# Weight tiles of 512 decoded in place, a 16-pair lag of the MoE behind the scores, three r tiles, and an output product moved ahead of a chunk's first product

## The chip, the cores and the metric

The kernel runs on one core of a Trainium2 chip. The metric is device time in microseconds (us), the median of three runs. In the text PE is TensorE (matmuls), PEld its weight loads, DVE is VectorE, ACT is ScalarE, POOL is GpSimd and SP is SyncE, whose queue issues every DMA of this kernel. Each engine works through its own instructions in order, and semaphores make one wait for another.

## The reference

Attention with squared ReLU in place of a softmax, gated by `u`, and behind it a mixture-of-experts block with one expert (RMS norm, SiLU gate, value projection, output projection):

```python
def _attn_ref(u, v, z):                 # batch 4, seq 3008, d_model 256, d_qk 64
    scores = (1.0 / S) * np.matmul(z, z.transpose(0, 2, 1))
    attn = np.maximum(scores, 0.0) ** 2
    return (u * np.matmul(attn, v)).astype(np.float32)

def _moe_ref(x, w_gate, w_val, w_out, rms_g):     # 12032 tokens, d_ff 1536
    rms = np.sqrt(np.mean(x * x, axis=-1, keepdims=True) + 1e-06)
    xn = x / rms * rms_g
    g = xn @ w_gate
    silu = g * (1.0 / (1.0 + np.exp(-g)))
    return (silu * (xn @ w_val) @ w_out).astype(np.float32)
```

The three weight matrices are float64 in the inputs; `u`, `v`, `z` are float32.

## The kernel before

**Tiling.** Of each batch's 3008 tokens, 512 make a chunk (five of 512 and one of 448: 24 chunks in all), and 128 make a k-tile (24, the last one half full). A *step* is one pair of chunk and k-tile; there are 576, and one loop runs over them (line 590). All products are made of two-part numbers, high and low: a step's attention product is six matmuls into `po` (`emit_av`, lines 353, 354, 358), a score is two (`emit_s`, lines 297, 298).

**A step.** The scores of step i+3 (LA = 3 ahead) go to PSUM; ACT takes the ReLU into a tile `r` (line 300; two such tiles). Then either ACT squares it twice, once rounded into `H` and once in place (lines 315, 316), or DVE multiplies it by the PSUM scores (line 302) and ACT rounds it into `H` (318); `is_square` says which. DVE subtracts to get the low part `L` (321). The scores are symmetric: for blocks that `keeps` names, ACT writes the square's halves out (334) and a later chunk reads them back turned, by a DMA transpose into tiles `T`, and needs no score matmuls for them.

**Chunk border.** Behind a chunk's last step, DVE multiplies `po` by `u` (`emit_gate`, 375). The next chunk's first product writes the same two `po` banks, so it waits for that. Thirteen small stages of the RMS norm (`norm_jobs`) follow, one in each step.

**MoE.** It trails the scores by `NK // 2 + SKEW` pairs of steps, SKEW = 8: in an even step six matmuls of the gate projection (`emit_g`, 464 to 467) and ACT's SiLU into the one `s` tile (474), in an odd step six of the value projection, then DVE's product `s` (483), ACT's `hH` (484) and DVE's `hL` (485). The output product `py` of the pair before (`emit_y`, 498 to 500) comes in even steps behind `emit_av`. There are 288 such pairs; those that are left when attention ends make the tail.

**Weights.** They come as pairs of 32-bit words (the float64's halves) in 36 tiles of 256 columns, 256 KB each. ACT takes a square (130), DVE runs three operations on the high words (134 to 138) and two more (143, 145), ACT rounds (146), and POOL makes the low part (147, 148). `load_w` finds a tile for each load among places that are free by then. They are planned from step 1 on, one in three steps, then in two, then in each.

**Order.** All instructions stand in program order as the loop emits them; `stages` and `loads` are lists by step. The loads of `v` and `z` use the `raw` ring (three tiles), in the first chunks with other tiles as well, and are planned four or five steps ahead.

Of the kernel before, what the change touches and what calls it, by code (L numbers as in the profile page):

```python
# [24 lines left out]

WC = 256
LEAST = 1.125 * 2.0 ** -15
# [3 lines left out]
def kernel(  # L31
# [25 lines left out]
    LA = 3  # L57
    SKEW = 8

    AHEAD = 5  # L60
    RAW = 3
    SCALE = 1.0 / S
# [35 lines left out]


    wraw_tags = [f"x{a}{d}{k}" for k in range(2) for a in "hl" for d in range(ND)] + ["raw"] * RAW  # L100
    w_queue = []

    def load_w(i):

        while w_queue and w_queue[0][0] <= i + AHEAD:
            at, load = w_queue[0]

            free = [t for t in wraw_tags if t == "raw" or at + 2 < (int(t[-1]) + 1) * NK + 11]
            if not free:
                assert at > i + 1, "no room"  # L110
                return
            w_queue.pop(0)
            load(free[0])

    def prep_w(src, hi, lo):

        tiles = {}

        def load(tag):
            wraw_tags.remove(tag)
            raw = work.tile([P, WC, 2], U32, tag=tag, name="wraw", bufs=RAW if tag == "raw" else 1)
            nc.sync.dma_start(out=raw.rearrange("p a b -> p (a b)"), in_=src.bitcast(U32))
            tiles["raw"] = raw, tag

        def magnitude(i):

            tiles["t"] = work.tile([P, WC], U32, tag="wt", name="wt", bufs=3)
            nc.scalar.activation(lo, f32(tiles["raw"][0][:, :, 1]), AF.Square)  # L130

        def upper(i):
            wh, t = tiles["raw"][0][:, :, 1], tiles["t"]
            nc.vector.tensor_scalar(t, wh, 3, 0x3FFFFFF8, op0=ALU.logical_shift_left, op1=ALU.bitwise_and)
            yield
            nc.vector.scalar_tensor_tensor(t, wh, 0xC0000000, t, op0=ALU.bitwise_and, op1=ALU.bitwise_or)
            yield
            nc.vector.scalar_tensor_tensor(f32(t), f32(lo), LEAST * LEAST, f32(t), op0=ALU.is_ge, op1=ALU.mult)

        def lower(i):  # L140
            (raw, tag), t = tiles["raw"], tiles["t"]
            wl, m = raw[:, :, 0], raw[:, :, 1]
            nc.vector.tensor_scalar(m, t, 0xFF800000, None, op0=ALU.bitwise_and)
            yield
            nc.vector.scalar_tensor_tensor(f32(m), wl, 2.0 ** -52, f32(m), op0=ALU.mult, op1=ALU.mult)
            nc.scalar.copy(hi, f32(t))
            nc.gpsimd.tensor_tensor(f32(t), f32(t), f32(hi), op=ALU.subtract)
            nc.gpsimd.tensor_tensor(lo, f32(t), f32(m), op=ALU.add)
            wraw_tags.append(tag)
            wraw_tags.sort(key=lambda t: t[-1])  # L150

        return load, [magnitude, upper, lower]


# [4 lines left out]

    rings = {True: ["raw", "T", "hH", "T", "hL"], False: ["raw"]}  # L160

    def new_raw(first):

        ring = rings[first]
        ring.append(ring.pop(0))
        if ring[-1] == "T":
            return work.tile([P, 2 * CH], F32, tag="T", name="raw", bufs=3)[:, :CH]
        return work.tile([P, CH], F32, tag=ring[-1], name="raw", bufs=RAW if ring[-1] == "raw" else 1)

# [19 lines left out]
    def prep_stat(b, c):  # L189
        t0 = c * CH  # L190
        n = min(CH, S - t0)
        m = n + TAIL if n < CH else n
        lo = slice(DQK, P)
        tiles = {}

        def load(i):
            raw = tiles["raw"] = new_raw(b == 0)
            nc.sync.dma_start(out=raw[:, :n], in_=zT2[:, b * S + t0:b * S + t0 + n])
            if n < m:
                nc.sync.dma_start(out=raw[:, n:m], in_=zT2[:, (b + 1) * S - TAIL:(b + 1) * S])  # L200

        def high(i):
            raw = tiles["raw"]
            z = keep.tile([P, CH], F32R, tag=f"zst{c}", name=f"zst{c}")
            nc.scalar.copy(z[:DQK, :m], raw[:DQK, :m])
            nc.vector.tensor_copy(z[lo, :m], raw[lo, :m])
            zst[b, c] = z

        def low(i):
            z = zst[b, c]  # L210
            nc.vector.tensor_tensor(z[lo, :m], tiles["raw"][lo, :m], f32(z[lo, :m]), op=ALU.subtract)

        return load, [high, low]

# [20 lines left out]
    def prep_v(b, g):  # L235
# [12 lines left out]

        def high(i):
            hi = vh[b, g] = keep.tile([P, 2, D], F32R, tag=f"vh{g}", name=f"vh{g}")  # L250
            nc.vector.tensor_copy(hi, tiles["raw"])

        def low(i):
            lo = vl[b, g] = keep.tile([P, 2, D], F32R, tag=f"vl{g}", name=f"vl{g}")
            nc.vector.tensor_tensor(lo, tiles["raw"], f32(vh[b, g]), op=ALU.subtract)  # L255

        return load, [high, low]

# [8 lines left out]
    def keeps(b, c, kc):  # L267


        return (b * NC + c) * NK + 4 * kc >= NK + 2 * SKEW  # L270

# [15 lines left out]
    def emit_s(i):  # L287
# [10 lines left out]
        nc.tensor.matmul(ps[:, :n], z[:, ks], ml[:, :n], start=False, stop=True)  # L298
        a = work.tile([P, CH], F32, tag="r", name="r", bufs=2)
        nc.scalar.activation(a[:, :n], ps[:, :n], AF.Relu)  # L300
# [4 lines left out]
    def is_square(i):  # L305

        return i < 2 * NK + 2 * SKEW and i % 4 != 3

    def emit_l(i):
# [19 lines left out]
        if kc > c and keeps(b, c, kc):  # L329
            if kt % 4 == 0:  # L330
                kept[b, kc, c] = dram.tile([2 * CH, CH], U16, tag=f"kept{kc}{c}", name=f"kept{kc}{c}")
            m = P if kt < NK - 1 else TAIL
            halves = work.tile([P, 2, CH], U16, tag="halves", name="halves", bufs=2)
            nc.scalar.copy(halves[:m], a[:m].bitcast(U16).rearrange("p (q h) -> p h q", h=2))  # L334
            r0 = 2 * (kt % 4) * P
            nc.sync.dma_start(
                out=kept[b, kc, c][r0:r0 + 2 * m, :].rearrange("(p h) q -> p h q", h=2), in_=halves[:m]
            )
# [138 lines left out]
    def emit_v(ci, f):  # L477
        n = chunks[ci][3]
        ps = proj(ci, f, wvh, wvl)
        h = moe["s"]  # L480
        hi = work.tile([P, CH], F32R, tag="hH", name="hH")
        lo = work.tile([P, CH], F32R, tag="hL", name="hL")
        nc.vector.tensor_tensor(h[:, :n], ps[:, :n], h[:, :n], op=ALU.mult)  # L483
# [6 lines left out]
    def emit_y(ci, f):  # L490
# [10 lines left out]
        if f == NF - 1:  # L501
            for d in range(ND):
                y = work.tile([P, CH], F32, tag=f"q{d}", name="y")
                if d == 0:
# [7 lines left out]

    nsteps = len(steps)
    loads = defaultdict(list)
# [8 lines left out]
    for g in range(NK // 2):  # L523
        if g % 2 == 0 and g // 2 + 1 < NC:
            plan(prep_stat(0, g // 2 + 1), 2 * g - 2, AHEAD)
        if g > 1:
            plan(prep_v(0, g), 2 * g - 3, AHEAD)
    at = 1
    for j in range(DFF // WC):
        js = slice(j * WC, (j + 1) * WC)  # L530
        group = []
        for src, hi, lo in ((w_gate, wgh, wgl), (w_val, wvh, wvl)):
            for d in range(ND):
                group.append((src[d * P:(d + 1) * P, js], hi[:, d, js], lo[:, d, js]))
        for f in range(j * WC // P, (j + 1) * WC // P):
            group.append((w_out[f * P:(f + 1) * P, :], woh[:, f, :], wol[:, f, :]))
        for w in group:
            load, parts = prep_w(*w)
            w_queue.append((at, load))
            for k, part in enumerate(parts):  # L540
                stages[at + k].append(part)
            at += 3 if at < NK else 2 if at < NK + 2 * SKEW - 2 else 1
    for ci in range(1, len(chunks)):

        first = next(i for i in range(ci * NK, (ci + 1) * NK) if not is_turned(i))
        plan(prep_mov(ci), max(ci * NK - LA - 1, first - LA - 4), 4)
    for i in range(0, len(steps), 2):
        if is_turned(i):
            loads[i - LA - 3].append(lambda at, i=i: load_turned(i))
    for b in range(1, batch):  # L550
        first = b * NC * NK
        for c in range(NC):
            plan(prep_stat(b, c), first - NK + 4 * c + 3, 4)
        for g in range(NK // 2):
            plan(prep_v(b, g), first - NK + 2 * g + 2, 4)

# [13 lines left out]
    with tc.manual_schedule():  # L570
# [4 lines left out]
        for i in sorted(k for k in loads if k < 0):  # L575
            run(loads, i)
        load_w(0)
        prep_const()
# [11 lines left out]
        for i in range(nsteps + 2 * (SKEW + NF + 1)):  # L590
# [11 lines left out]
            run(loads, i)  # L602
            load_w(i)
            m = moe_at(fs)
            if m:
                if i % 2 == 0:
                    emit_g(*m)
                else:
                    emit_v(*m)
            if i < nsteps:  # L610
                emit_av(i)
            m = moe_at(fs - 1)
            if m and i % 2 == 0:
                emit_y(*m)
# [39 lines left out]
```

## Time and profile before

| | before |
|---|---|
| median of 3 runs | 2247.09 us (2246.83 to 2247.13) |
| profiled execution | 2247.23 us, its span 2245.5 us |
| granted PE clock over the span | 0.995 |
| matmuls | 9368 |
| DMA | 166.78 MB, mean 74 GB/s |
| ACT's largest wait for a matmul chain: `hH` for `s` | 567.1 us |

The busy shares overlap. A busy PE is not one at its peak, since each matmul's recorded time covers part of the next one's; how far apart matmuls start says more. Idle time counts only on the engine that sets the pace of its stretch. Names such as `po<-H,vh` mean: tile `po` is written, from `H` and `vh`.

### The profile page before, as it was taken

Reading aid. Unit: us, or ns where it says so; the run is one execution under the profiler, and the core shown is the slowest. Engines: PE = TensorE matmul, PEld = TensorE weight load, DVE = VectorE, ACT = ScalarE, POOL = GpSimd, SP = SyncE. Lnnn points to the kernel's source line nnn. Section 1 sums busy time; section 2 is a strip of 40 time slices with the busy share of each in tenths; the row PEclk is TensorE's granted clock in tenths of the full one; section 3 lists DMA queues with packets and bytes.
Section 4 is the critical chain, followed back from the end, with each engine's and each line's share of the span. In section 5 each row is a group of like instructions: output and inputs, shape, how many; then the busy total and the mean of one; then the engine's idle time right before and its main releaser. Section 6 shows DMA issues by size and latency. Waiting matters only on the chain.

```text
span 2245.5 us, 25802 instructions
## 1 busy us (share of the span) xinstructions
PE 2180.1 (97%) x9368; PEld 1748.5 (78%) x9368; DVE 1321.8 (59%) x2416; ACT 1167.9 (52%) x1994; POOL 61.6 (3%) x76
## 2 busy tenths in 40 slices
PE   7789999999999999999999999999999999999998
PEld 4456787888888878788788787788888877877876
DVE  7668655567555555557656555556755565555442
ACT  6676645444656455344566463544465655544332
POOL 1233000000000000000000000000000000000000
PEclk9999999999999999999999999999999999999999
DMA  4131303152223142334131332415222314133200
GB/s 137 38 101 43 96 15 86 47 115 70 88 56 110 43 101 61 78 91 109 63 97 57 77 93 48 109 47 119 82 80 64 114 38 106 53 82 77 63 0 18
DMA packets 280016, 166.78 MB, mean 74 GB/s; under 512 B 218640, under 2 KB 234128, under 8 KB 279888
## 3 DMA queue, kind: packets, MB, share of 16 engines
q1 hardware_dynamic: 279888, 165.13, 28.0%
q8 instruction: 73, 1.20, 0.2%
q14 instruction: 55, 0.45, 0.1%
HBM read 46.60 MB, written 65.40 MB: 50 GB/s over the span
## 4 chain that ended last, share of the span: by engine, by line
PE 86%; DVE 6%; ACT 5%; issue 2%; DMA 0%; POOL 0%; DVEq 0%; ACTq 0%; SPq 0%; POOLq 0%
PE ps L464 11%; PE ps L465 10%; PE ps L467 10%; PE po L353 10%; PE po L354 10%; PE po L358 10%; PE py L498 6%; PE py L500 6%; PE py L499 6%; PE ps L297 3%; PE ps L298 3%; DVE L L321 2%; DVE s L483 1%; ACT hH L484 1%; ACT r L300 1%
## 5 line engine op out<-in xcount | busy, mean ns | idle before, releaser
L353 PE MATMUL po<-H,vh 128*128 128x512 f32 (+1 forms) x1152 | 458.9, 398 | 23.6 <-DVE ux L375 13.4
L484 ACT CAST hH<-s 128x512 fp32r<-128x512 f32 (+1 forms) x288 | 176.4, 612 | 567.1 <-DVE s L483 567.1
L354 PE MATMUL po<-H,vl 128*128 128x512 f32 (+1 forms) x1152 | 452.2, 393 | 0.3 <-DVE vl L255 0.3
L302 DVE TENSOR_TENSOR r<-ps,r 128x512 f32<-128x512 f32 (+1 forms) x316 | 216.6, 686 | 322.5 <-ACT r L300 321.8
L300 ACT ACTIVATE r<-ps 128x512 f32<-128x512 f32 (+1 forms) x364 | 216.4, 595 | 345.5 <-PE ps L298 244.8
L358 PE MATMUL po<-L,vh 128*128 128x512 f32 (+1 forms) x1104 | 344.1, 393 | 10.1 <-DVE L L321 10.1
L483 DVE TENSOR_TENSOR s<-ps,s 128x512 f32<-128x512 f32 (+1 forms) x288 | 194.6, 676 | 237.5 <-PE ps L467 237.1
L485 DVE TENSOR_TENSOR hL<-s,hH 128x512 fp32r<-128x512 f32 (+1 forms) x288 | 196.2, 681 | 198.9 <-ACT hH L484 198.9
L353 PEld LDWEIGHTS po<-H,vh 128*128 128x128 f32 x1152 | 217.4, 189 | 94.8 <-ACT H L318 22.1
L321 DVE TENSOR_TENSOR L<-r,H 128x512 fp32r<-128x512 f32 (+1 forms) x340 | 237.7, 699 | 46.9 <-ACT r L316 23.8
L358 PEld LDWEIGHTS po<-L,vh 128*128 128x128 f32 x1104 | 205.8, 188 | 63.8 <-DVE L L321 20.2
L354 PEld LDWEIGHTS po<-H,vl 128*128 128x128 f32 x1152 | 217.5, 189 | 45.9 <-DVE vl L255 1.5
L498 PE MATMUL py<-hH,woh 128*128 128x512 f32 (+1 forms) x576 | 228.6, 397 | 14.4 <-ACT hH L484 13.6
L500 PE MATMUL py<-hL,woh 128*128 128x512 f32 (+1 forms) x576 | 228.4, 396 | 0.0
L464 PE MATMUL ps<-xh,wgh 128*128 128x512 f32 (+1 forms) x576 | 226.2, 393 | 1.6 <-ACT s L474 1.6
L464 PE MATMUL ps<-xh,wvh 128*128 128x512 f32 (+1 forms) x576 | 224.6, 390 | 0.0
L465 PE MATMUL ps<-xh,wvl 128*128 128x512 f32 (+1 forms) x576 | 224.6, 390 | 0.0
L334 ACT COPY halves<-r 128x1024 uint16<-128x1024 uint16 x212 | 222.1, 1047 | 4.4 <-DMA kept<-halves 4.2
L499 PE MATMUL py<-hH,wol 128*128 128x512 f32 (+1 forms) x576 | 224.1, 389 | 0.0
L465 PE MATMUL ps<-xh,wgl 128*128 128x512 f32 (+1 forms) x576 | 224.0, 389 | 0.0
L474 ACT ACTIVATE s<-ps 128x512 f32<-128x512 f32 (+1 forms) x288 | 169.9, 590 | 101.8 <-PE ps L467 74.1
L318 ACT CAST H<-r 128x512 fp32r<-128x512 f32 (+1 forms) x316 | 192.5, 609 | 0.6 <-DVE small L409 0.3
(81 smaller groups left out, 2713.0 us busy)
## 6 DMA issues: line engine op xcount, KB each, us to landing
kept<-halves SPq DMA_DIRECT2D x193, 256.0 KB, 2.0
raw<-in_v SPq DMA_DIRECT2D x44, 256.0 KB, 3.3
ux<-in_uT SPq DMA_DIRECT2D x40, 256.0 KB, 2.8
out_T<-y SPq DMA_DIRECT2D x40, 256.0 KB, 2.0
raw<-in_zT SPq DMA_DIRECT2D x39, 256.0 KB, 2.9
wraw<-in_w_gate SPq DMA_DIRECT2D x12, 256.0 KB, 3.1
wraw<-in_w_val SPq DMA_DIRECT2D x12, 256.0 KB, 2.7
wraw<-in_w_out SPq DMA_DIRECT2D x12, 256.0 KB, 3.1
```

The source lines that it names most:

```text
L300: nc.scalar.activation(a[:, :n], ps[:, :n], AF.Relu)
L321: nc.vector.tensor_tensor(lo[:, :n], a[:, :n], f32(hi[:, :n]), op=ALU.subtract)
L334: nc.scalar.copy(halves[:m], a[:m].bitcast(U16).rearrange("p (q h) -> p h q", h=2))
L353: nc.tensor.matmul(po[d][:, :n], wh[:, j, ds], hi[:, :n], start=(kt == 0), stop=False)
L354: nc.tensor.matmul(po[d][:, :n], wl[:, j, ds], hi[:, :n], start=False, stop=(lo is None))
L358: nc.tensor.matmul(po[d][:, :n], wh[:, j, ds], lo[:, :n], start=False, stop=False)
L464: nc.tensor.matmul(ps[:, :n], hi[:, d, fs], xsplit[ci, d][0][:, :n], start=(d == 0), stop=False)
L465: nc.tensor.matmul(ps[:, :n], lo[:, d, fs], xsplit[ci, d][0][:, :n], start=False, stop=False)
L467: nc.tensor.matmul(ps[:, :n], hi[:, d, fs], xsplit[ci, d][1][:, :n], start=False, stop=(d == ND - 1))
L498: nc.tensor.matmul(py[d][:, :n], woh[:, f, ds], hi[:, :n], start=(f == 0), stop=False)
L499: nc.tensor.matmul(py[d][:, :n], wol[:, f, ds], hi[:, :n], start=False, stop=False)
L500: nc.tensor.matmul(py[d][:, :n], woh[:, f, ds], lo[:, :n], start=False, stop=(f == NF - 1))
```

## The change

- **Weights**: 18 tiles of 512 columns (512 KB each) in place of 36 of 256, decoded in the tile itself, at a stride of two words, with one scratch tile `wt`. They take turns on the three `T` tiles and are loaded three steps ahead. The first is due at step 4; one follows every 5 steps up to step 59, then every 2 up to step 71.
- **SKEW** goes from 8 to 16: the MoE begins at step 56 in place of 40, and 28 pairs stand in the tail in place of 20. `keeps` begins at NK + 3·SKEW = 72 in place of 40, which takes out five blocks of batch 0 (20 scores are computed that had been read back turned). `is_square` covers steps up to 80 and two of three steps, in place of 64 and three of four.
- **Tiles**: `r` three in place of two; `raw` two in place of three, with loads of later batches planned two steps ahead in place of four; `halves` and `y` share two tiles; from the tail on `hH` and `hL` use the three `H` and `L` tiles.
- **Splits** of `v` and `z` take one step in place of two.
- **Output product**: in a chunk's first step `emit_y` comes ahead of `emit_av`; in the tail it comes behind the value projection in place of the gate projection.

```diff
-WC = 256
+WC = 512
...
-    SKEW = 8
+    SKEW = 16
...
-    RAW = 3
+    RAW = 2
...
-    wraw_tags = [f"x{a}{d}{k}" for k in range(2) for a in "hl" for d in range(ND)] + ["raw"] * RAW
-    def load_w(i):
...
     def prep_w(src, hi, lo):
+        a, b = hi.shape[1:]
...
-        def load(tag):
-            wraw_tags.remove(tag)
-            raw = work.tile([P, WC, 2], U32, tag=tag, name="wraw", bufs=RAW if tag == "raw" else 1)
-            nc.sync.dma_start(out=raw.rearrange("p a b -> p (a b)"), in_=src.bitcast(U32))
-            tiles["raw"] = raw, tag
+        def load(i):
+            raw = work.tile([P, a, b, 2], U32, tag="T", name="wraw", bufs=3)
+            nc.sync.dma_start(out=raw.rearrange("p a b c -> p a (b c)"), in_=src.bitcast(U32))
+            tiles["wl"], tiles["wh"] = raw[:, :, :, 0], raw[:, :, :, 1]
+        def new_t():
+            return work.tile([P, WC], U32, tag="wt", name="wt").rearrange("p (a b) -> p a b", a=a)
         def magnitude(i):
-            tiles["t"] = work.tile([P, WC], U32, tag="wt", name="wt", bufs=3)
-            nc.scalar.activation(lo, f32(tiles["raw"][0][:, :, 1]), AF.Square)
+            nc.scalar.activation(hi, f32(tiles["wh"]), AF.Square)
         def upper(i):
-            wh, t = tiles["raw"][0][:, :, 1], tiles["t"]
+            wh, t = tiles["wh"], new_t()
...
-            nc.vector.scalar_tensor_tensor(t, wh, 0xC0000000, t, op0=ALU.bitwise_and, op1=ALU.bitwise_or)
-            yield
-            nc.vector.scalar_tensor_tensor(f32(t), f32(lo), LEAST * LEAST, f32(t), op0=ALU.is_ge, op1=ALU.mult)
+            nc.vector.scalar_tensor_tensor(wh, wh, 0xC0000000, t, op0=ALU.bitwise_and, op1=ALU.bitwise_or)
+            yield
+            nc.vector.scalar_tensor_tensor(f32(wh), f32(hi), LEAST * LEAST, f32(wh), op0=ALU.is_ge, op1=ALU.mult)
         def lower(i):
-            (raw, tag), t = tiles["raw"], tiles["t"]
-            wl, m = raw[:, :, 0], raw[:, :, 1]
-            nc.vector.tensor_scalar(m, t, 0xFF800000, None, op0=ALU.bitwise_and)
-            yield
-            nc.vector.scalar_tensor_tensor(f32(m), wl, 2.0 ** -52, f32(m), op0=ALU.mult, op1=ALU.mult)
-            nc.scalar.copy(hi, f32(t))
-            nc.gpsimd.tensor_tensor(f32(t), f32(t), f32(hi), op=ALU.subtract)
-            nc.gpsimd.tensor_tensor(lo, f32(t), f32(m), op=ALU.add)
-            wraw_tags.append(tag)
-            wraw_tags.sort(key=lambda t: t[-1])
+            wh, wl, t = tiles["wh"], tiles["wl"], new_t()
+            nc.vector.tensor_scalar(t, wh, 0xFF800000, None, op0=ALU.bitwise_and)
+            yield
+            nc.vector.scalar_tensor_tensor(f32(wl), wl, 2.0 ** -52, f32(t), op0=ALU.mult, op1=ALU.mult)
+            nc.scalar.copy(hi, f32(wh))
+            nc.gpsimd.tensor_tensor(f32(wh), f32(wh), f32(hi), op=ALU.subtract)
+            nc.gpsimd.tensor_tensor(lo, f32(wh), f32(wl), op=ALU.add)
...
-    rings = {True: ["raw", "T", "hH", "T", "hL"], False: ["raw"]}
+    rings = {True: ["raw", "hH", "raw", "hL"], False: ["raw"]}
     def new_raw(first):
...
-        if ring[-1] == "T":
-            return work.tile([P, 2 * CH], F32, tag="T", name="raw", bufs=3)[:, :CH]
...
     def prep_mov(ci):
...
     def keeps(b, c, kc):
-        return (b * NC + c) * NK + 4 * kc >= NK + 2 * SKEW
+        return (b * NC + c) * NK + 4 * kc >= NK + 3 * SKEW
     def is_turned(i):
...
-        a = work.tile([P, CH], F32, tag="r", name="r", bufs=2)
+        a = work.tile([P, CH], F32, tag="r", name="r", bufs=3)
...
     def is_square(i):
-        return i < 2 * NK + 2 * SKEW and i % 4 != 3
+        return i < 2 * NK + 2 * SKEW and i % 3 != 2
     def emit_l(i):
...
-            halves = work.tile([P, 2, CH], U16, tag="halves", name="halves", bufs=2)
+            halves = work.tile([P, 2, CH], U16, tag="out", name="halves", bufs=2)
...
-        hi = work.tile([P, CH], F32R, tag="hH", name="hH")
-        lo = work.tile([P, CH], F32R, tag="hL", name="hL")
+        own = 2 * (ci * NF + f + NK // 2 + SKEW) < nsteps
+        hi = work.tile([P, CH], F32R, tag="hH" if own else "H", name="hH", bufs=1 if own else LA)
+        lo = work.tile([P, CH], F32R, tag="hL" if own else "L", name="hL", bufs=1 if own else LA)
...
-                y = work.tile([P, CH], F32, tag=f"q{d}", name="y")
+                y = work.tile([P, CH], F32, tag="out", name="y", bufs=2)
...
-    nsteps = len(steps)
...
-            plan(prep_stat(0, g // 2 + 1), 2 * g - 2, AHEAD)
+            plan(prep_stat(0, g // 2 + 1), 2 * g - 1, AHEAD)
...
-            plan(prep_v(0, g), 2 * g - 3, AHEAD)
-    at = 1
+            plan(prep_v(0, g), 2 * g - 2, AHEAD)
+    at = 4
...
+        fs = slice(j * WC // P, (j + 1) * WC // P)
...
-                group.append((src[d * P:(d + 1) * P, js], hi[:, d, js], lo[:, d, js]))
-        for f in range(j * WC // P, (j + 1) * WC // P):
-            group.append((w_out[f * P:(f + 1) * P, :], woh[:, f, :], wol[:, f, :]))
+                group.append((src[d * P:(d + 1) * P, js].unsqueeze(1), hi[:, d:d + 1, js], lo[:, d:d + 1, js]))
+        for f in range(fs.start, fs.stop, 2):
+            rows = w_out[f * P:(f + 2) * P, :].rearrange("(a p) d -> p a d", p=P)
+            group.append((rows, woh[:, f:f + 2, :], wol[:, f:f + 2, :]))
...
-            load, parts = prep_w(*w)
-            w_queue.append((at, load))
-            for k, part in enumerate(parts):
-                stages[at + k].append(part)
-            at += 3 if at < NK else 2 if at < NK + 2 * SKEW - 2 else 1
+            plan(prep_w(*w), at, 3)
+            at += 5 if at < NK + 2 * SKEW else 2
...
-        plan(prep_mov(ci), max(ci * NK - LA - 1, first - LA - 4), 4)
+        plan(prep_mov(ci), max(ci * NK - LA - 1, first - LA - 4), 2)
...
-            plan(prep_stat(b, c), first - NK + 4 * c + 3, 4)
+            plan(prep_stat(b, c), first - NK + 4 * c + 3, 2)
...
-            plan(prep_v(b, g), first - NK + 2 * g + 2, 4)
+            plan(prep_v(b, g), first - NK + 2 * g + 2, 2)
     def moe_at(fs):
...
-        load_w(0)
...
-            load_w(i)
...
+            m = moe_at(fs - 1)
+            y_first = i < nsteps and kt == 0
+            if m and y_first:
+                emit_y(*m)
...
-            m = moe_at(fs - 1)
-            if m and i % 2 == 0:
+            if m and not y_first and i % 2 == (0 if i < nsteps else 1):
...
```

How it moves instructions, at three places. First PE at a chunk's border in the middle of the program (`ps<-xl,wgh` ends the gate projection, `po` is the new chunk's first product, `py` the output product). Before:

```order
L467 MATMUL ps<-xl_10445,wgh 128x512
L353 MATMUL po_10881<-H,vh_8531 128x512
L354 MATMUL po_10881<-H,vl_8566 128x512
L353 MATMUL po_10882<-H,vh_8531 128x512
L354 MATMUL po_10882<-H,vl_8566 128x512
L358 MATMUL po_10881<-L,vh_8531 128x512
L358 MATMUL po_10882<-L,vh_8531 128x512
L498 MATMUL py_10711<-hH,woh 128x512
```

And with the change:

```order
L444 MATMUL ps<-xl_9273,wgh 128x448
L477 MATMUL py_10048<-hH,woh 128x448
L478 MATMUL py_10048<-hH,wol 128x448
L479 MATMUL py_10048<-hL,woh 128x448
L477 MATMUL py_10049<-hH,woh 128x448
L478 MATMUL py_10049<-hH,wol 128x448
L479 MATMUL py_10049<-hL,woh 128x448
L330 MATMUL po_10500<-H,vh_8142 128x512
L331 MATMUL po_10500<-H,vl_8144 128x512
```

The six `py` matmuls stand between the gate projection and the first writer of `po`.

Second, PE in the tail (`wgh` is the gate projection, `wvh` and `wvl` the value projection). Before:

```order
L467 MATMUL ps<-xl_18436,wgh 128x448
L467 MATMUL ps<-xl_18439,wgh 128x448
L498 MATMUL py_18551<-hH,woh 128x448
L499 MATMUL py_18551<-hH,wol 128x448
L500 MATMUL py_18551<-hL,woh 128x448
L498 MATMUL py_18552<-hH,woh 128x448
L499 MATMUL py_18552<-hH,wol 128x448
L500 MATMUL py_18552<-hL,woh 128x448
L464 MATMUL ps<-xh_18435,wvh 128x448
```

And with the change:

```order
L444 MATMUL ps<-xl_18049,wgh 128x448
L444 MATMUL ps<-xl_18052,wgh 128x448
L441 MATMUL ps<-xh_18048,wvh 128x448
L442 MATMUL ps<-xh_18048,wvl 128x448
L441 MATMUL ps<-xh_18051,wvh 128x448
L442 MATMUL ps<-xh_18051,wvl 128x448
L444 MATMUL ps<-xl_18049,wvh 128x448
L444 MATMUL ps<-xl_18052,wvh 128x448
L477 MATMUL py_18400<-hH,woh 128x448
```

`py` has moved behind the value projection.

Third, DVE in the first chunk, around the decoding of the first weight tile (`wt` and `wraw`; `L` and `r` belong to the scores, `zst`, `vh` and `vl` to the splits). Before:

```order
L134 TENSOR_SCALAR wt<-wraw 128x256
L136 SCALAR_TENSOR_TENSOR wt<-wraw,wt 128x256
L138 SCALAR_TENSOR_TENSOR wt<-wgl,wt 128x256
L321 TENSOR_TENSOR L<-r,H 128x512
L211 TENSOR_TENSOR zst_196<-raw,zst_196 64x512
L251 CAST vh_225<-raw 128x512
L143 TENSOR_SCALAR wraw<-wt 128x256
L145 SCALAR_TENSOR_TENSOR wraw<-wraw 128x256
```

And with the change:

```order
L121 TENSOR_SCALAR wt<-wraw 128x512
L123 SCALAR_TENSOR_TENSOR wraw<-wraw,wt 128x512
L125 SCALAR_TENSOR_TENSOR wraw<-wgh,wraw 128x512
L298 TENSOR_TENSOR L<-r,H 128x512
L230 CAST vh_276<-raw 128x512
L232 TENSOR_TENSOR vl_278<-raw,vh_276 128x512
L129 TENSOR_SCALAR wt<-wraw 128x512
L131 SCALAR_TENSOR_TENSOR wraw<-wraw,wt 128x512
```

The same five operations are twice as wide, write into the raw tile, and both halves of a `v` split stand together.

More of the change, by code (lines that the diff above doesn't have):

```diff
@@ L76 @@
     steps = [(ci, kt) for ci in range(len(chunks)) for kt in range(NK)]
+    nsteps = len(steps)
     def f32(ap):
@@ L97, in prep_const @@
         nc.sync.dma_start(out=fold_sb, in_=fold)
-    wraw_tags = [f"x{a}{d}{k}" for k in range(2) for a in "hl" for d in range(ND)] + ["raw"] * RAW
-    w_queue = []
-    def load_w(i):
[L105 to L113, printed above, removed]
@@ L200, in load, with split @@
                 nc.sync.dma_start(out=raw[:, n:m], in_=zT2[:, (b + 1) * S - TAIL:(b + 1) * S])
-        def high(i):
+        def split(i):
             raw = tiles["raw"]
@@ L206, in high @@
             nc.vector.tensor_copy(z[lo, :m], raw[lo, :m])
+            nc.vector.tensor_tensor(z[lo, :m], raw[lo, :m], f32(z[lo, :m]), op=ALU.subtract)
             zst[b, c] = z
[L209 to L213, printed above, removed]
+        return load, [split]
     def prep_first():
@@ L247, in load, with split @@
                     nc.sync.dma_start(out=view[h * TAIL:(h + 1) * TAIL, 1, :], in_=v[r0 + P:r0 + P + TAIL, :])
-        def high(i):
+        def split(i):
             hi = vh[b, g] = keep.tile([P, 2, D], F32R, tag=f"vh{g}", name=f"vh{g}")
             nc.vector.tensor_copy(hi, tiles["raw"])
-        def low(i):
             lo = vl[b, g] = keep.tile([P, 2, D], F32R, tag=f"vl{g}", name=f"vl{g}")
             nc.vector.tensor_tensor(lo, tiles["raw"], f32(vh[b, g]), op=ALU.subtract)
-        return load, [high, low]
+        return load, [split]
     att = {}
```

## The prediction

> **What bounds the kernel now.** I read the page first, then busy time by stretches, then groups and waits inside the slow stretch, then the timeline at a chunk's border and at the end.
>
> ```profile
> PE 2180.1 (97%) x9368; PEld 1748.5 (78%) x9368; DVE 1321.8 (59%) x2416; ACT 1167.9 (52%) x1994; POOL 61.6 (3%) x76
> PE 86%; DVE 6%; ACT 5%; issue 2%; DMA 0%; POOL 0%; DVEq 0%; ACTq 0%; SPq 0%; POOLq 0%
> ```
>
> PE's 97% is no measure of how full it is, because a matmul's busy time overlaps the next one's. The spacing of starts is the measure:
>
> ```profile
> 2151.16 0.39 PE L464 MATMUL ps<-xh,wvh 128*128 128x512 f32 x1
> 2151.39 0.40 PE L465 MATMUL ps<-xh,wvl 128*128 128x512 f32 x1
> ...
> 75.20 0.63 PE L354 MATMUL po<-H,vl 128*128 128x512 f32 x1
> 75.63 0.63 PE L353 MATMUL po<-H,vh 128*128 128x512 f32 x1
> ```
>
> A full 512-wide matmul occupies 0.233 us at full clock, and 0.43 us where the clock was halved. With 0.233 I weigh five stretches, cut at the first `po` product of steps 0, 24, 40 and 64 and near the end of attention:
>
> ```profile
> core 0: us, PE busy (x) PEld busy (x) DVE busy (x) ACT busy (x) POOL busy (x), PEclk, DMA share, GB/s
> 8.87:83.13 74.26, 59.00 (x192) 34.82 (x191) 53.41 (x102) 47.05 (x89) 12.69 (x14) 0.95 0.26 84
> 83.13:132.28 49.15, 37.49 (x137) 24.38 (x138) 34.48 (x78) 30.80 (x60) 11.37 (x14) 0.97 0.17 53
> 132.28:248.96 116.68, 103.28 (x404) 76.92 (x403) 93.58 (x192) 80.96 (x155) 37.31 (x44) 0.96 0.24 76
> 248.96:2158.50 1909.54, 1897.33 (x8307) 1551.75 (x8306) 1105.75 (x1982) 981.37 (x1645) 0.00 (x0) 1.00 0.30 76
> ```
>
> 192 matmuls (24 steps of 8) are worth 44.7 us and took 74.3: 29.5 over. The next two rows are 49.2 − 31.9 = 17.2 and 116.7 − 94.1 = 22.5 over. So 69 us are lost before step 64. The long fourth row has 8307 matmuls at 0.230 us each, with the 448-wide ones among them: PE is full there, and only a small regular wait is left. The kernel is therefore bound by PE, except in its first 250 us, at chunk borders, and in its tail.
>
> In the first 40 steps (3.09 us each, with 1.87 us of matmuls) neither DVE (87.9 of 123.4 us) nor ACT (77.9) is full. They wait for each other:
>
> ```profile
> L300 ACT ACTIVATE r<-ps 128x512 f32<-128x512 f32 x25 | 15.0, 599 | 26.6 <-DVE L L321 25.5 <-PE ps L298 1.1
> L321 DVE TENSOR_TENSOR L<-r,H 128x512 fp32r<-128x512 f32 x24 | 18.1, 753 | 14.9 <-ACT r L316 12.2 <-ACT H L318 2.4
> ACT r L300 <- DVE L L321: 43.5, 39, 3.1
> PE ps L297 <- DVE mh L181: 4.5, 1, 4.5
> ```
>
> The first two rows are groups of steps 0–23, the last two are waits of steps 0–39. With two `r` tiles, the ReLU of a step has to wait until DVE has taken `L` from the `r` of two steps earlier: 43.5 us in 39 waits.
>
> **The change part by part.** The profiled execution took 2247.23 us (span 2245.5), 0.14 above the median shown; the sum starts from 2247.2.
>
> *(1) The start: three `r` tiles, bigger weight tiles, MoE 16 steps later.* The third `r` tile moves that wait a whole step back, so I let it go. What is late next is DVE itself. A weight tile costs DVE two `tensor_scalar` and three `scalar_tensor_tensor`, at these prices:
>
> ```profile
> L136 DVE SCALAR_TENSOR_TENSOR wt<-wraw,wt 128x256 uint32<-128x256 uint32 x8 | 3.4, 425 | 0.3
> L134 DVE TENSOR_SCALAR wt<-wraw 128x256 uint32<-128x256 uint32 x8 | 2.3, 288 | 0.0
> L181 DVE TENSOR_SCALAR mh<-raw 128x512 fp32r<-128x512 f32 x19 | 8.0, 419 | 0.0
> L183 DVE SCALAR_TENSOR_TENSOR ml<-raw,mh 128x512 fp32r<-128x512 f32 x19 | 13.1, 692 | 1.4
> L136 DVE SCALAR_TENSOR_TENSOR wt<-wraw,wt 128x256 uint32<-128x256 uint32 x21 | 13.1, 623 | 0.0
> 180.00:200.00 20.00, 18.20 (x77) 13.54 (x76) 18.23 (x38) 11.86 (x26) 7.67 (x9) 1.00 0.19 62
> ```
>
> At 256 wide that is 2 × 0.288 + 3 × 0.425 = 1.85 us; at 512 wide, by the rows of `mh` and `ml`, 2 × 0.42 + 3 × 0.69 = 2.91. No row shows the 512-wide form written in place at a stride of two words. From below it is bounded by 2.91. From above I take the stretched form, since the fifth row (steps 40–63) shows the same instruction at 623 ns where DVE and POOL are both loaded: 2 × 0.42 + 3 × 1.02 = 3.9. In the sparse start I use 2.91, as the 256-wide forms, two of them strided, run unstretched there.
>
> DVE's work in the new steps 0–55: the 87.9 us of the old steps 0–39, less 15 old tiles (27.8), plus 16 more `L` (11.0), about 9 more `r` products as `is_square` and its span change (6.0), one more `mh`/`ml` pair (1.1), most of chunk 1's gate and norm (7), plus 11 new tiles (32.0): 117 us. ACT has less. The last row shows how full DVE gets where it leads: 91%. That gives 129 us. Run step by step without any slack (a heavy step of DVE never overlapping a heavy one of ACT) I come to about 148. I take 140, nearer the middle, because LA lets engines drift by a step or two but the border at step 24 (the 4.5 us wait for `mh`) keeps part of its cost. 56 steps are 448 matmuls, 104.4 us: 35.6 over.
>
> Steps 56–72 then carry MoE and the last 7 weight tiles. DVE: 17 `L` (11.7), 6 `r` products (4), 7 tiles at 2.9 to 3.9 (20 to 27), 17 MoE operations (11.6), norms (4): 52 to 59 us. PE: 17 steps of about 17 matmuls, 67 us. PE leads, with little room; I allow 5. Together 40.6 over in place of 69.3: **−28.7**, between −40 (129 us and no loss behind) and −17 (148 us, 8 behind).
>
> POOL's two operations double in width and halve in number; ACT's too. They lie beside this. The weight loads grow to 512 KB and are issued three steps ahead:
>
> ```profile
> wraw<-in_w_gate SPq DMA_DIRECT2D x12, 256.0 KB, 3.1
> ```
>
> Three steps are 7 us in the start, and twice the 3.1 us of a 256 KB load is 6.2 at most, so I cost them at nothing; were each 3 us late, DVE would have L and v work to go on with.
>
> *(2) The output product ahead of a chunk's first product.*
>
> ```profile
> PE po L353 <- DVE ux L375: 13.4, 19, 1.3
> 1262.03 0.69 DVE L485 TENSOR_TENSOR hL<-s,hH 128x512 fp32r<-128x512 f32 x1 [0.69 <-ACT hH L484]
> 1262.25 0.64 PE L467 MATMUL ps<-xl,wgh 128*128 128x512 f32 x2
> 1262.64 1.28 DVE L375 TENSOR_TENSOR ux<-po,ux 128x512 f32<-128x512 f32 x2
> 1263.47 0.47 PE L353 MATMUL po<-H,vh 128*128 128x512 f32 x1 [0.58 <-DVE ux L375]
> ```
>
> DVE takes the gate only after `hL`; PE runs out of matmuls at 1262.72 and starts `po` at 1263.47. Six `py` matmuls put in there take 1.4 us, to 1264.1, past the gate's first half. Their own input `hL` is done at 1262.72, and the first reader of it stands third. So the wait goes: **−13.4**. Borders 24 and 48 have no MoE work and keep theirs. If `py` waited as long as `po` does now, the term would be zero.
>
> *(3) The tail: `py` behind both projections.*
>
> ```profile
> 2199.93 0.62 DVE L483 TENSOR_TENSOR s<-ps,s 128x448 f32<-128x448 f32 x1 [2.44 <-PE ps L467]
> 2201.19 0.62 DVE L485 TENSOR_TENSOR hL<-s,hH 128x448 fp32r<-128x448 f32 x1 [0.63 <-ACT hH L484]
> 2201.21 0.47 PE L498 MATMUL py<-hH,woh 128*128 128x448 f32 x1 [0.18 <-ACT hH L484]
> 2201.91 0.55 ACT L474 ACTIVATE s<-ps 128x448 f32<-128x448 f32 x1 [0.75 <-DVE hL L485]
> 2204.27 0.62 DVE L483 TENSOR_TENSOR s<-ps,s 128x448 f32<-128x448 f32 x1 [2.46 <-PE ps L467]
> 2238.03 0.36 PE L465 MATMUL ps<-xh,wvl 128*128 128x448 f32 x1
> 2238.23 0.56 PE L467 MATMUL ps<-xl,wvh 128*128 128x448 f32 x2
> 2240.18 0.47 PE L498 MATMUL py<-hH,woh 128*128 128x448 f32 x1 [1.38 <-ACT hH L484]
> ```
>
> A pair takes 4.34 us where its 18 matmuls need 18 × 0.200 = 3.6, since `py` stands right behind the next gate product and needs an `hH` that is just being made. 12 pairs lose 0.74 and 8 wider ones about 0.5; the last loses 1 more: 13.9. In the new order `py` comes one more projection and one more `py` later (2.4 us), beyond `hL`. The loop over the one `s` tile (L483 to the end of L474) takes 2.5 us and fits into 3.6. There are 28 pairs now in place of 20, all at PE's pace. The very last `py` still waits some 0.4: **−13.5**, and zero at worst.
>
> *(4) Fewer kept scores.* `keeps` asks for 72 where it asked for 40, so five blocks of batch 0 are computed and not turned: 40 more matmuls, 24 of 512 and 16 of 448 (0.233 and 0.200 us), all in the stretch where PE is full: **+8.8**. ACT loses 20 `halves` copies, DVE gains 20 products; both are half idle there.
>
> Sum: 2247.2 − 28.7 − 13.4 − 13.5 + 8.8 = **2200**.
>
> **A rule against the row.** Short spells of half clock lie in the start; one is in this row:
>
> ```profile
> 120.00:130.00 10.00, 6.75 (x21) 4.18 (x22) 6.23 (x12) 5.37 (x12) 2.97 (x4) 0.83 0.33 106
> 121.11 0.50 PE L353 MATMUL po<-H,vh 128*128 128x512 f32 x1 [1.67 <-ACT H L315]
> ```
>
> The Trainium skill, "TensorE: Matmul & The Clock Gate", section "HAM oscillation — how this bites in real kernels", has it that only PE gaps above about 3.4 us throttle the array. By that rule shorter gaps would end all spells and (1) would sit nearer its −40. The trace differs: here the clock fell with no PE wait above 1.67 us in the row, so I count no gain from it.
>
> **Rivals.**
> - *The start stays as it is* (13%): ACT and DVE remain in lockstep for other reasons, and 56 steps go at 3.09 us, 173 us, 69 over. Term (1) is zero: 2229. For it: three waits of different kinds stand in that stretch. Against it: 43.5 us of one kind, with DVE at 71% and ACT at 63%.
> - *`py` or its tile inherits the border's wait* (6%): term (2) is zero: 2213.
> - *Half clock through the attention-only steps* (3%): 8 × 0.43 = 3.4 us a step, 190 us in place of 140: 2250, no change. Against it: PE is busier there than before, and the clock was 0.95 and 0.97.
> - *Slower: late `v` and `z` loads at the three changes of batch* (5%). `raw` has two tiles in place of three and loads are planned two steps ahead in place of four, on SP's queue, where a load waiting for its tile holds up all behind it. One takes 3.3 us:
>
> ```profile
> raw<-in_v SPq DMA_DIRECT2D x44, 256.0 KB, 3.3
> ```
>
> 54 loads exposed by half of that cost 89 us: 2289. It decides from 0.96 us each (52 us over the forecast). Two steps of 3.73 us (1909.5 us over 512 steps) leave 4.1 us beyond the landing, so a load is exposed only where its tile comes free a whole step after it was asked for; by the due times that is one load at each change. Hence the small chance.
>
> **How the numbers follow.** The forecast has 73% and its own range 2184 to 2214 (term (1) from −40 to −17, and a few us for borders and tail). Reaching into the first rival, 2184 to 2225 leaves out about 2 in 10: most of that rival, the last two, and a little below. This kernel's runs can tell about 0.2%, 4.5 us, from no change. Faster: forecast, first two rivals, 92%; same 3%; slower 5%.
>
> **What would show it.** Right: the wait of `r` for `L` nearly gone; DVE near 85–90% busy in the first 56 steps, with step 56 near 150 us; no wait of `po` for `ux` after step 72; tail pairs at 3.6 us. Wrong: step 56 near 180 us; `py` waiting at borders for `hL`; DVE waiting for `raw` in a batch's last chunk; PE clock near 0.5 early.

## The result, and the profile after

The changed kernel takes 2186.56 us (median of 4 runs, 2185.81 to 2187.04) against 2247.11 us; the ratio is 0.9731, 95% interval 0.9714 to 0.9747. That is 60.6 us less, where 47 were forecast. The profiled execution took 2186.13 us. Its page begins:

```profile
span 2184.4 us, 25522 instructions
PE 2152.9 (99%) x9408; PEld 1763.3 (81%) x9408; DVE 1321.7 (61%) x2340; ACT 1161.1 (53%) x1964; POOL 55.2 (3%) x40
PE 92%; DVE 5%; ACT 1%; issue 1%; DMA 1%; SPq 0%; DVEq 0%; ACTq 0%
```

PE has 40 matmuls more, and its share of the chain that ended last went from 86% to 92%. Busy time by stretches, cut at the first `po` product of steps 0, 24, 56 and 72 and near the end of attention (columns as before):

```profile
8.90:69.33 60.43, 49.05 (x191) 35.89 (x191) 55.70 (x87) 45.13 (x82) 12.47 (x8) 0.97 0.39 122
69.33:146.08 76.75, 66.75 (x265) 50.78 (x265) 66.47 (x115) 58.59 (x105) 18.47 (x12) 0.96 0.17 57
146.08:210.96 64.88, 64.13 (x272) 50.08 (x270) 53.56 (x82) 42.38 (x76) 20.87 (x14) 1.00 0.17 54
210.96:2066.00 1855.04, 1854.46 (x8151) 1525.68 (x8150) 1092.99 (x1966) 973.47 (x1633) 3.14 (x2) 1.00 0.29 75
```

At 0.233 us a matmul the first three are 15.9, 15.0 and 1.5 us over, 32.4 together; before, 69.3 were lost by step 64. DVE is busy for 122.2 of the 137.2 us of steps 0 to 55, 89%. Step 56 began at 146.1 us (about 149 forecast). In the fourth row PE is busy for all but 0.6 us. The start's two groups (steps 0 to 55), and the wait of `po` for the gate, over the whole run:

```profile
L277 ACT ACTIVATE r<-ps 128x512 f32<-128x512 f32 x58 | 34.3, 592 | 24.0 <-DVE L L298 13.7 <-PE ps L275 9.8
L298 DVE TENSOR_TENSOR L<-r,H 128x512 fp32r<-128x512 f32 x56 | 50.5, 909 | 10.7 <-ACT r L293 6.7 <-ACT H L295 3.9
PE po L330 <- DVE ux L352: 1.8, 1, 1.8
```

ACT's idle time for `L` fell from 43.5 us in 40 steps to 13.7 in 56, and of 19 waits of `po` for the gate one is left, before the MoE begins. One number was not expected: an `L` takes 909 ns here, where it takes 690 elsewhere.

In the tail a pair of 448 columns now takes 3.60 us, which is 18 matmuls of 0.200 us, as `s` shows on the timeline:

```profile
2141.81 0.62 DVE L462 TENSOR_TENSOR s<-ps,s 128x448 f32<-128x448 f32 x1 [0.94 <-PE ps L444]
2145.41 0.62 DVE L462 TENSOR_TENSOR s<-ps,s 128x448 f32<-128x448 f32 x1 [1.72 <-PE ps L444]
```

### The profile page after: what moved, and what is told of

The parts are those of the page before. It is cut to its first block, busy times and chain, and to the rows that moved or that the text cites. A ratio compares the mean times of both kernels' runs of the same rounds, so it can differ in the third digit from the quotient of the medians.

```text
span 2184.4 us, 25522 instructions
## 1 busy us (share of the span) xinstructions
PE 2152.9 (99%) x9408; PEld 1763.3 (81%) x9408; DVE 1321.7 (61%) x2340; ACT 1161.1 (53%) x1964; POOL 55.2 (3%) x40
## 4 chain that ended last, share of the span: by engine, by line
PE 92%; DVE 5%; ACT 1%; issue 1%; DMA 1%; SPq 0%; DVEq 0%; ACTq 0%
PE ps L441 12%; PE ps L444 12%; PE ps L442 12%; PE po L330 11%; PE po L331 11%; PE po L335 10%; PE py L479 6%; PE py L477 6%; PE py L478 6%; PE ps L275 4%; PE ps L274 4%; DVE L L298 1%; DVE r L279 0%; ACT r L277 0%; DVE wraw L123 0%
## 5 line engine op out<-in xcount | busy, mean ns | idle before, releaser
L330 PE MATMUL po<-H,vh 128*128 128x512 f32 (+1 forms) x1152 | 452.2, 393 | 2.8 <-DVE ux L352 1.8
L279 DVE TENSOR_TENSOR r<-ps,r 128x512 f32<-128x512 f32 (+1 forms) x330 | 225.4, 683 | 335.4 <-ACT r L277 332.2
L277 ACT ACTIVATE r<-ps 128x512 f32<-128x512 f32 (+1 forms) x384 | 227.4, 592 | 323.8 <-PE ps L275 300.8
L298 DVE TENSOR_TENSOR L<-r,H 128x512 fp32r<-128x512 f32 (+1 forms) x360 | 260.2, 724 | 27.8 <-ACT H L295 15.2
L311 ACT COPY halves<-r 128x1024 uint16<-128x1024 uint16 x192 | 201.1, 1048 | 3.5 <-DMA out_T<-y 3.5
L295 ACT CAST H<-r 128x512 fp32r<-128x512 f32 (+1 forms) x330 | 200.7, 608 | 0.2 <-PE po L331 0.2
```

The costliest lines, as they stand in the source:

```text
L279: nc.vector.tensor_tensor(a[:, :n], ps[:, :n], a[:, :n], op=ALU.mult)
L298: nc.vector.tensor_tensor(lo[:, :n], a[:, :n], f32(hi[:, :n]), op=ALU.subtract)
L330: nc.tensor.matmul(po[d][:, :n], wh[:, j, ds], hi[:, :n], start=(kt == 0), stop=False)
```

## The experiments

Each kernel is the changed one with one change, except the second, which is the kernel before with one. 1 to 9 were run once each, 10 to 12 four times; the four runs of a kernel lie within 0.9 to 2.2 us.

**1. Two `r` tiles again.**

```diff
-        a = work.tile([P, CH], F32, tag="r", name="r", bufs=3)
+        a = work.tile([P, CH], F32, tag="r", name="r", bufs=2)
```

> The changed kernel with two r tiles in place of three, nothing else. Theory A (the third r tile is what frees the start; ReLU waits for DVE's L without it): the steps before the MoE go back towards the old 3.1 us, so step 56 starts some 20 to 35 us later than its 146 us and the whole is 2205 to 2220 us, with the wait of r for L back at 40 us or more before step 56. Rival S (the later MoE and the sparser weight tiles freed the start): step 56 stays within 5 us of 146 and the whole within 2185 to 2192 us.

2234.86 us: 48.3 more than the changed kernel, which leaves 12 of the 60.6 us. Step 56 begins at 184.4 us. Groups up to there:

```profile
L277 ACT ACTIVATE r<-ps 128x512 f32<-128x512 f32 x57 | 34.1, 598 | 71.1 <-DVE L L298 64.7 <-PE ps L275 4.1 <-DVE H L303 1.5
L298 DVE TENSOR_TENSOR L<-r,H 128x512 fp32r<-128x512 f32 x55 | 45.0, 817 | 41.4 <-ACT r L293 27.3 <-ACT H L295 14.0
```

The wait is back at 64.7 us, and `L` waits for ACT in turn. Theory A holds, and the cost exceeds its 20 to 35 us: 175.5 us for 56 steps is 3.13 us a step, the old pace, paid 16 steps longer because the MoE starts later; nearly 9 us more are lost between steps 56 and 72.

**2. Three `r` tiles in the kernel before.**

```diff
-        a = work.tile([P, CH], F32, tag="r", name="r", bufs=2)
+        a = work.tile([P, CH], F32, tag="r", name="r", bufs=3)
...
-        t = work.tile([P, 2, 2 * CH], U16, tag="T", name="T", bufs=3)
+        t = work.tile([P, 2, 2 * CH], U16, tag="T", name="T", bufs=2)
...
```

> The kernel before with three r tiles; to make room the T tiles are two in place of three, which can slow the turned blocks later on, so only the start is read, up to step 40 (132.3 us before). Theory A: the wait of r for L falls from 43.5 us to under 15 us and step 40 starts 15 to 25 us earlier, at 107 to 117 us. Rival S: step 40 stays within 5 us of 132.

Step 40 begins at 107.8 us in place of 132.3, and the whole is 2220.03 us, 26.7 below the kernel before beside it. The two `T` tiles did no visible harm: from step 100 to the last step of attention it takes 1760.2 us, the kernel before 1760.1. The group of the ReLU up to step 40:

```profile
L300 ACT ACTIVATE r<-ps 128x512 f32<-128x512 f32 x41 | 24.2, 589 | 9.0 <-PE ps L298 5.1 <-DVE L L321 3.6
```

The wait for `L` is 3.6 us in place of 43.5, as theory A has it. So one tile more brings 26.7 us alone, and the start's other edits about 10 on top of it (37 against 26.7).

**3. The output product behind the first product again.**

```diff
-            y_first = i < nsteps and kt == 0
+            y_first = False
```

> The changed kernel with the output product behind the chunk's first attention product again. By term (2) of the prediction the wait of po for ux comes back at 21 borders, 0.65 to 0.75 us each: 13 to 16 us, 2199 to 2202 us in all. Rival (the border's wait is gone for another reason, such as another alignment of MoE chunks to attention chunks): within 3 us of 2186.

2204.85 us, 18.3 more, and over the whole run this wait:

```profile
PE po L330 <- DVE ux L352: 17.4, 21, 1.8
```

The mechanism is as forecast. Two of the 21 waits (1.08 and 1.77 us) stand at the borders of steps 24 and 48, ahead of the MoE, where the edit changes nothing; the other 19 are 14.6 us, within the 13 to 16 expected. That the whole loses 18.3 is because a recorded wait is only a part of what PE loses at a border, as one of them shows:

```profile
1293.94 0.62 PE L444 MATMUL ps<-xl,wgh 128*128 128x512 f32 x2
1295.19 0.47 PE L330 MATMUL po<-H,vh 128*128 128x512 f32 x1 [0.63 <-DVE ux L352]
1295.50 0.40 PE L331 MATMUL po<-H,vl 128*128 128x512 f32 x1
```

The second matmul of the first row starts at about 1294.17, and `po` 1.02 us behind it in place of 0.23; the next one follows 0.31 later. Some 0.9 us are lost where a wait of 0.63 is recorded.

**4. The old order in the tail.**

```diff
-            if m and not y_first and i % 2 == (0 if i < nsteps else 1):
+            if m and not y_first and i % 2 == 0:
```

> The changed kernel with the output product behind the gate projection in the tail again, as before. By term (3) each of the 28 pairs in the tail loses 0.5 (512 wide) to 0.74 us (448 wide), about 17 to 20 us: 2203 to 2207 us. Rival (the tail's gain comes from the H and L tiles that hH and hL now use there): within 3 us of 2186.

2207.15 us, 20.6 more. The period of `s` in this tail is 4.31 us:

```profile
2151.31 0.62 DVE L462 TENSOR_TENSOR s<-ps,s 128x448 f32<-128x448 f32 x1 [0.58 <-PE ps L444]
2152.58 0.47 PE L477 MATMUL py<-hH,woh 128*128 128x448 f32 x1 [0.18 <-ACT hH L463]
2155.62 0.62 DVE L462 TENSOR_TENSOR s<-ps,s 128x448 f32<-128x448 f32 x1 [2.44 <-PE ps L444]
```

The tiles alone, which this kernel keeps, bring almost nothing (4.31 us in place of 4.34 before); the order does. Whether the new order would do as well without them was not run.

**5. DVE's decoding in halves of 256 columns.**

```diff
+            for k in range(2):
+                wh, t, h = half(whole, k), half(scratch, k), half(hi, k)
...
```

> The changed kernel with each of DVE's five decoding operations done on two halves of 256 columns, one after the other. Theory W (what is left of the start's gain, some 9 us beyond the third r tile, is DVE time that the wide tiles save): a tile costs DVE 3.7 in place of 2.9 us, 11 tiles stand before step 56, so step 56 starts 7 to 10 us later than 146 us and the whole is 2193 to 2198 us. Rival K (it is the later MoE, which leaves more room per weight tile): step 56 within 3 us of 146, the whole 2185 to 2190 us.

Step 56 begins at 153.0 us, 6.9 later, and the whole is 2196.96 us, 10.4 more; another 4.2 us are lost between steps 56 and 72. Both are what theory W expected, with DVE busy for 127.8 us up to step 56 in place of 122.2.

**6. SKEW 8 with the other edits kept.**

```diff
-    SKEW = 16
+    SKEW = 8
...
-            at += 5 if at < NK + 2 * SKEW else 2
+            at += 4 if at < NK + 2 * SKEW else 2
```

> The changed kernel with SKEW 8 again (MoE from step 40, 20 pairs in the tail), weight tiles every 4 steps up to step 40 and every 2 behind it, and the bounds of keeps (72) and is_square (80) held where the change puts them. Theory W: DVE has the same work in either order, the whole is within 6 us of 2186. Rival K: the 9 us go back, 2193 to 2200 us, with waits of PE for woh, wol, wgh or wvh or a fuller DVE between steps 40 and 60.

2192.54 us, 6.0 more: at the edge of W's range and below K's. PE waits for no weight tile up to step 56; `py` waits 3.9 us for `hH`. Both seem to count; W's 10.4 (experiment 5) and these 6 are more than the 10 us there are, so they are not independent. This stays undecided.

**7. One POOL operation per tile in place of two.**

```diff
-            nc.gpsimd.tensor_tensor(f32(wh), f32(wh), f32(hi), op=ALU.subtract)
```

> The changed kernel without POOL's subtraction in the decoding, so that the low half of each weight is wrong; POOL has one operation per tile (1.4 us) in place of two (3.1 us). DVE's L averages 909 ns before step 56 where 690 is usual. Theory P (DVE operations that start while POOL works stand until POOL is done): L falls to 770 to 830 ns and step 56 starts 4 to 8 us earlier, 2178 to 2183 us in all. Rival (L is stretched by something else, such as the loads): L stays near 900 ns and step 56 within 2 us of 146.

This kernel leaves the subtraction out, which changes the weights' values. 2175.66 us, 10.9 less; step 56 begins at 138.2 us.

```profile
L297 DVE TENSOR_TENSOR L<-r,H 128x512 fp32r<-128x512 f32 x56 | 41.6, 748 | 12.6 <-ACT r L292 7.0 <-ACT H L294 5.3
```

More than theory P expected. The changed kernel's timeline shows how DVE is held:

```profile
24.68 0.69 DVE L131 SCALAR_TENSOR_TENSOR wraw<-wraw,wt 128x512 f32<-128x512 uint32 x1
24.79 1.73 POOL L133 TENSOR_TENSOR wraw<-wraw,wgh 128x512 f32<-128x512 f32 x1 [24.35 <-DVE wt L129]
25.29 1.78 DVE L298 TENSOR_TENSOR L<-r,H 128x512 fp32r<-128x512 f32 x1
26.60 1.37 POOL L134 TENSOR_TENSOR wgl<-wraw 128x512 fp32r<-128x512 f32 x1
27.10 1.15 DVE L188 CAST zst<-raw 64x512 fp32r<-64x512 f32 x1
28.29 0.69 DVE L189 TENSOR_TENSOR zst<-raw,zst 64x512 fp32r<-64x512 f32 x1
```

`L` starts in the middle of POOL's subtraction (to 26.52) and ends 0.55 us behind it; the cast starts in POOL's addition (to 27.97) and ends 0.28 behind that. Of the 56 `L` before step 56, 15 began during a POOL operation and average 1519 ns, the other 41 average 686. POOL is held in turn: its subtraction, which here begins in DVE's L131, takes 1.73 us, and the only one in the trace that met no DVE operation takes 1.32.

**8. POOL's two operations on DVE.**

```diff
-            nc.gpsimd.tensor_tensor(f32(wh), f32(wh), f32(hi), op=ALU.subtract)
-            nc.gpsimd.tensor_tensor(lo, f32(wh), f32(wl), op=ALU.add)
+            nc.vector.tensor_tensor(f32(wh), f32(wh), f32(hi), op=ALU.subtract)
+            nc.vector.tensor_tensor(lo, f32(wh), f32(wl), op=ALU.add)
```

> The changed kernel with POOL's subtraction and addition of the decoding done by DVE. Theory P: DVE gets 1.38 us more work per tile (15 us before step 56) but loses the standing behind POOL (L 909 to 690 ns, 12 us, and some 3 us on other operations), so step 56 stays within 4 us of 146 and the whole is 2183 to 2191 us, with L near 690 ns. Rival (POOL's hold is a small matter, and the missing subtraction helped in another way): DVE's extra 15 us show, step 56 near 158 and the whole 2196 to 2202 us.

2186.99 us, step 56 at 146.5: no difference, with this group:

```profile
L298 DVE TENSOR_TENSOR L<-r,H 128x512 fp32r<-128x512 f32 x55 | 37.5, 687 | 12.6 <-ACT r L293 6.9 <-ACT H L295 4.4 <-PE ps L275 1.0
```

So all that POOL took off DVE was paid back by holding it.

**9. More squares on ACT.**

```diff
-        return i < 2 * NK + 2 * SKEW and i % 3 != 2
+        return i < 2 * NK + 2 * SKEW and i % 6 != 5
```

> The changed kernel with five of six early steps squared on ACT in place of two of three, which takes 9 or 10 products (0.69 us) from DVE before step 56 and gives ACT 0.65 us each. Theory D (DVE sets the start's pace): step 56 starts 3 to 6 us earlier than 146 us, the whole 2180 to 2183 us. Rival (ACT and DVE in turn set it, as in the step-by-step sum of the prediction): step 56 within 2 us of 146 or later.

2186.88 us, step 56 at 148.0. DVE's busy time up to there fell from 122.2 to 116.8 us, yet nothing was won:

```profile
L298 DVE TENSOR_TENSOR L<-r,H 128x512 fp32r<-128x512 f32 x55 | 50.2, 920 | 19.4 <-ACT r L293 16.8 <-ACT H L295 2.4 <-PE ps L275 0.2
```

`L` now waits 16.8 us for ACT's square in place of 6.7. Theory D fails in its plain form.

**10. POOL's operations in four pieces.**

```diff
...
-            nc.gpsimd.tensor_tensor(f32(wh), f32(wh), f32(hi), op=ALU.subtract)
-            nc.gpsimd.tensor_tensor(lo, f32(wh), f32(wl), op=ALU.add)
+            for k in range(4):
+                nc.gpsimd.tensor_tensor(f32(part(wh, k)), f32(part(wh, k)), f32(part(hi, k)), op=ALU.subtract)
+                nc.gpsimd.tensor_tensor(part(lo, k), f32(part(wh, k)), f32(part(wl, k)), op=ALU.add)
```

> The changed kernel with each of POOL's two operations per weight tile done in four pieces of 128 columns, alternating. Theory H (a DVE operation with SBUF operands alone that starts while POOL works is held until that one POOL operation ends, whatever its length): shorter POOL operations hold DVE shorter, L before step 56 averages 720 to 800 ns in place of 909, step 56 starts 3 to 8 us earlier, 2178 to 2183 us in all. Rival (DVE is held for as long as POOL has work, or POOL's start costs eat the gain): L near 900 ns, step 56 within 2 us of 146.

2177.88 us (2177.18 to 2178.12), ratio 0.9691 (0.9674 to 0.9707); step 56 at 139.0: 8.7 us less, just below the 2178 expected. POOL itself is slower, 50.5 us up to there in place of 31. The last of these rows is the start's busy time, with its granted clock:

```profile
L304 DVE TENSOR_TENSOR L<-r,H 128x512 fp32r<-128x512 f32 x55 | 42.2, 775 | 12.2 <-ACT r L299 7.7 <-ACT H L301 4.4
L139 POOL TENSOR_TENSOR wraw<-wraw,wgh 128x128 f32<-128x128 f32 x16 | 11.6, 724 | 44.4 <-DVE wt L134 30.2 <-ACT H L298 7.2 <-ACT H L301 7.0
L140 POOL TENSOR_TENSOR wgl<-wraw 128x128 fp32r<-128x128 f32 x16 | 9.8, 615 | 1.3
8.90:138.00 129.10, 111.56 (x451) 81.67 (x451) 112.80 (x198) 102.79 (x185) 50.48 (x80) 1.00 0.28 90
```

Theory H holds: DVE is held to the end of one POOL operation, not for as long as POOL has work. The hold hurts, not POOL's total. A part of the gain may come by another way: the changed kernel's start ran at 0.97 and 0.96 of the clock, by which some 10 of its 137 us were at half clock, and this one ran at 1.00. That is worth at most 5 of the 8.7 us (an estimate from these rows); how much of it counts was not separated.

**11 and 12. Three of the five blocks turned again**, alone and with the quarters.

```diff
-        return (b * NC + c) * NK + 4 * kc >= NK + 3 * SKEW
+        return (b * NC + c) * NK + 4 * kc >= NK + 24
```

> The changed kernel with keeps from step 48 on in place of 72, so three of the five lost blocks are turned again: 24 matmul pairs less, 16 of 512 and 8 of 448 single matmuls, by term (4) 5.4 us of PE. It adds 12 halves copies of ACT (1.05 us each) in steps 60 to 71, where PE leads by little. Theory (PE leads there): 2180 to 2183 us. Rival (ACT and DVE, with decoding and MoE, cannot take the copies): 2184 to 2190 us, with PE waiting for H or L between steps 60 and 72.

2182.11 us (2181.97 to 2183.34), ratio 0.9711 (0.9695 to 0.9727): 4.5 of the 5.4 us of 24 matmuls (12 pairs, where the expectation says 24).

> The same with keeps from step 48 on. If the two act apart, as PE leads where the scores are saved and does not where POOL works, the gains add: 4.5 us beside those of the quarters, 2174 to 2179 us. If the decoding's last tiles, in steps 60 to 71, get in the way of the halves copies, they do not: 2178 to 2183 us.

2173.05 us (2172.00 to 2174.16), ratio 0.9669 (0.9655 to 0.9684). The gains add (8.7 and 4.8), and the time is 1 us below the range expected. This version is 74.1 us below the kernel before and 13.5 below the changed one.

## Why the prediction was right, and where it was off

The direction, the three places and their mechanisms were right. The time lies in the range, near its lower end, since all four terms came out better than forecast:

| term | forecast | measured |
|---|---|---|
| (1) start | −28.7 | −36.9 (32.4 over in place of 69.3) |
| (2) border | −13.4 | −18.3 (the whole of experiment 3) |
| (3) tail | −13.5 | −14.7 (20.6 over 28 pairs, taken for 20) |
| (4) scores | +8.8 | +7.4 (4.5 for 24 matmuls, taken for 40) |

The four measured terms come from different comparisons and add up to 62.5 us, 2 more than the 60.6 of the whole.

- **The start's cause was right.** The wait of ReLU for `L` was the one to remove: the third `r` tile alone is worth 26.7 us in the old layout (2) and 48.3 in the new (1). The first rival, that the steps stay at 3.09 us, is what the change becomes without it: 3.13.
- **Its size was off in two steps, both too cautious.** "Steps 56–72 ... I allow 5": 1.5 were lost. "I take 140" for 56 steps, 35.6 over: 137.2, 30.9 over. The lower bound of the term was added up wrongly: 129 us and no loss behind give −44.7, not −40. The wait of `r` for `L` was to be "nearly gone" and is 13.7 us. And the way to 140 was wrong. "What is late next is DVE itself" holds only in part: taking 5 us from DVE and giving 5 to ACT changed nothing (9), so the two set the pace in turn, which is what the step-by-step bound of 148 supposed.
- **"POOL's two operations ... lie beside this" was wrong.** DVE's 122.2 us of the start, forecast 117, hold about 12 us in which `L` stood behind POOL (56 times 909 less 687 ns). Its trace stood in the prediction: the mean of 753 ns for `L` and the 623 ns that I took for general load. In the trace of before, 6 of those 24 `L` began during a POOL operation and average 943 ns, the others 690; 8 of the 21 operations at 623 ns did and average 962, the others 414. The Trainium skill, "SBUF — State Buffer", section "SBUF: two separate sides", calls the port pair of VectorE and GpSimd an exclusive lock that whichever instruction starts first holds to its end, for VectorE instructions with two SBUF inputs or in a two-port mode. The trace agrees: 1.78 us for an `L` that began in a POOL operation, and 0.68 for products that read PSUM. It holds POOL's operations too (1.73 us for the subtraction that began in one of DVE's, 1.32 for the one that met none).
- **The border's mechanism was right, its size read too low.** 13.4 us in 19 waits is recorded idle time, which is not all that PE loses. The prediction's own lines have PE out of matmuls at 1262.72 and starting at 1263.47, 0.75 us, where 0.58 are recorded. By the spacing of starts around the 18 borders from step 144 on, the kernel before lost about 17.8 us there with 12.1 recorded, and the changed kernel with the old order 18.5 with 12.8 (3). The two lose nearly the same, so another alignment of MoE chunks to borders plays little part.
- **The tail** followed the forecast's loop: pairs at 3.60 us, no wait for `s`.
- **The clock** may have given something where the prediction counted nothing. By the granted clock of the rows, about 20 us of the start were at half clock before (0.95, 0.97, 0.96) and about 10 with the change (0.97, 0.96, 1.00); that is worth up to 5 us of term (1), an estimate that no run separates. The rule that the prediction weighed (the Trainium skill, "TensorE: Matmul & The Clock Gate", section "HAM oscillation — how this bites in real kernels") would have left no spell in the changed kernel's start, where no wait of PE is over 2.6 us. The clock still fell to 0.83 in three stretches of 10 us there, so the trace's side was the right one. Experiment 10, with no wait over 1.9 us, ran its start at 1.00.
- **Late loads at batch changes** did not show: the fourth row of the stretches has PE busy for 1854.46 of 1855.04 us.

What stays open is how the start's last 10 us divide between wide tiles and the later MoE (5, 6).

## What to carry to other kernels

When two engines hand tiles to each other in turn, count the buffers between them first: here a third buffer was worth 26.7 us by itself, and without it the changed start is about 11 us slower than the old one (48.3 against 36.9). Put work that needs a finished chain behind other matmuls of the same queue, at a border and in a tail alike. An engine that is 3% busy can still set another's pace: look at the mean duration of the same instruction in different stretches before its work is costed at nothing.

## What the runs showed of the hardware

- An `L` that began during a POOL operation ended a fixed time behind it. In the changed kernel's trace 21 did so; they average 1489 ns, where the 315 of the same width that met no POOL operation average 681, and end about 0.55 us behind POOL's end. Nine products that read PSUM (two `r`, seven `s`) began during one too and took 680 ns as ever.
- POOL was held by DVE as well. In the same trace the subtraction took 1.76 us in the 17 cases that began during a DVE operation and 1.32 in the one that met none; the addition took 1.37 in 15 that began in a subtraction of DVE and 1.04 in the one that met no DVE operation.
- POOL's time does not scale with width: where they met no DVE operation, the two took 1.32 and 1.04 us at 512 columns, and 0.47 and 0.40 at 128 (10).
- A 512-column decode in place, at a stride of two words, cost DVE what a plain one does: 694 ns and 417 ns in the start, where `ml` and `mh` took 692 and 419.
